# Delta rule and top-1 MoE: all 32 heads per chunk in tiled matmuls, with 16x16 diagonal blocks solved on GpSimd

## The chip, the cores and the metric

The kernel runs on one core of one Trainium2 chip. The metric is the device time of one execution in microseconds (us); lower is better. Everything is computed in float32 except the integer-valued lists of the selection, which use bfloat16. Engines are named as the profile names them: PE is TensorE (matmuls), PEld its weight loads, DVE VectorE, ACT ScalarE, POOL GpSimd, SP the SyncE queue that issues most transfers. "L269" is line 269 of the kernel.

## The reference

Two stages follow each other. The first is a delta-rule attention over 4 batches, 8 heads, 768 tokens and head dimension 48; the second a mixture of 8 experts, in which every token goes to its best expert and every expert keeps at most 80 tokens, those with the highest gate weight.

```
    k_n = k / (np.linalg.norm(k, axis=-1, keepdims=True) + 1e-06)
    state = np.zeros((B, H, D, D), dtype=np.float32)
    y = np.zeros_like(q)
    for t in range(S):
        kt, vt, bt = (k_n[:, :, t], v[:, :, t], beta[:, :, t, None])
        y[:, :, t] = np.einsum('bhd,bhde->bhe', q[:, :, t], state)
        v_old = np.einsum('bhde,bhd->bhe', state, kt)
        state = state + bt[:, :, :, None] * np.einsum('bhd,bhe->bhde', kt, vt - v_old)
    return y.astype(np.float32)

# ── moe block (D resized to bridge) ──
_moe_kname = 'topk_capacity_drop'
# ...
    x = np.ascontiguousarray(attn_out.transpose(0, 2, 1, 3)).reshape(B * S, H * D)   # 3072 x 384
    logits = x @ w_gate
    expert_idx = np.argmax(logits, axis=1)
# ... softmax; gate_w = probability of the chosen expert
    for e in range(E):
        tok_idx = np.where(expert_idx == e)[0]
        if len(tok_idx) > capacity:                  # capacity is 80
# ...       keep the 80 tokens with the largest gate_w
        h = np.maximum(x[tok_idx] @ w1[e], 0.0)      # 384 -> 1024
        out[tok_idx] = gate_w[tok_idx, None] * (h @ w2[e])   # 1024 -> 384
```

The loop over tokens is not run as a loop. Tokens are taken in chunks of 64. Within a chunk, with A[t, s] = beta_s k_t.k_s for s < t and S the 48x48 state of a head, the kernel solves Z = (I + A)^-1 (V - K S), sets U = beta Z, returns y = Q S + (Q K^T, s < t) U, and adds K^T U to S. So a chunk of one head needs the inverse of a 64x64 unit-triangular matrix, which does not depend on S, and a short chain of products that does.

## The kernel before

Two heads share a 128x128 tile, block-diagonal over the pair; a step handles one batch, one chunk, and its four pairs. There are 4 x 12 = 48 such steps, taken two at a time. The inverse comes from blocks that double in size: five rounds of two 128x128 matmuls and a transpose, each round with two or three evictions from PSUM (the accumulator memory of PE).

```
            for n in range(1, len(widths)):                  # widths 1, 2, 4, ..., 32
                pp = pm_tile()
                for p in range(NP):
                    nc.tensor.matmul(pp[:, p, :], lhsT=B1[:, p, :], rhs=X[:, p, :], start=True, stop=True)
                P2 = mtile("P2", 3)
                nc.vector.tensor_tensor(out=P2, in0=pp, in1=over_pairs(masks[n]), op=Alu.mult)
                yield
                if n < len(widths) - 1:
                    px = pm_tile()
                    for p in range(NP):
                        nc.tensor.matmul(px[:, p, :], lhsT=Y[:, p, :], rhs=P2[:, p, :], start=True, stop=True)
                    X = mtile("X")
                    nc.scalar.copy(X, px)
                    yield
                py = pm_tile()
                for p in range(NP):
                    if n < len(widths) - 1:
                        nc.tensor.transpose(py[:, p, :], X[:, p, :], ident)
                    else:
                        nc.tensor.matmul(py[:, p, :], lhsT=P2[:, p, :], rhs=Y[:, p, :], start=True, stop=True)
                Y = mtile("Y", 5)
                nc.scalar.copy(Y, py)
                yield
```

Ahead of it stand the transposes of K and Q and the two Gram products (L241, L246, L248), and after it the chain that depends on the state:

```
                for p in range(NP):
                    nc.tensor.matmul(ps[:, p, :], lhsT=KT[:, p, :], rhs=st[:, p, :], start=True, stop=True)
                R = vec.tile([128, NP, D], F32, name="R")
                nc.vector.tensor_tensor(out=R, in0=vin[b][:, :, c, :], in1=ps, op=Alu.subtract)
                yield
            ps = pc_tile()[:, :PD].rearrange("q (p d) -> q p d", p=NP)
            for p in range(NP):
                nc.tensor.matmul(ps[:, p, :], lhsT=Y[:, p, :], rhs=R[:, p, :], start=True, stop=True)
            U = vec.tile([128, NP, D], F32, name="U")
            nc.vector.tensor_tensor(out=U, in0=ps, in1=beta_t[:, b, :, c : c + 1].to_broadcast([128, NP, D]),
                                    op=Alu.mult)
            yield
            py = pc_tile()[:, :PD].rearrange("q (p d) -> q p d", p=NP)
            for p in range(NP):
                if c > 0:
                    nc.tensor.matmul(py[:, p, :], lhsT=QT[:, p, :], rhs=state[b][:, p, :], start=True, stop=False)
                nc.tensor.matmul(py[:, p, :], lhsT=PT[:, p, :], rhs=U[:, p, :], start=(c == 0), stop=True)
# ...                                              state += kb^T U (L322); y to DRAM as x_rows (L334)
            r = slice(C * (c % 2), C * (c % 2) + C)
            for n in range(NP):
                g, e = divmod(n, 2)
                nc.tensor.matmul(pl[r, :E], lhsT=xT[:, g, 64 * e : 64 * e + 64], rhs=wg[:, g, e, :],
                                 start=(n == 0), stop=(n == NP - 1))
            nc.vector.tensor_copy(lg[r, b * NT + c // 2, :], pl[r, :E])
```

When a batch is finished its gate weights are formed on DVE (L356 to L388), and the 80 largest of each expert are kept in lists. A list here is the tokens of one 128-token tile for one expert, 6 x 8 = 48 lists of 80 kept and 128 new values. After the last batch the 48 lists are brought to one row per expert by six transfers and searched again:

```
            for t in range(TR):
                m8 = nx[:, t * 8 : t * 8 + 8]
                nc.vector.max(m8, cd)
                nc.vector.match_replace(cd, in_to_replace=m8, in_values=cd, imm_value=0.0)
                if t % 2:
                    yield
# ... after the last batch
        mg = sl.tile([E, NT, CW], F32, name="mg")
        for t in range(NT):
            nc.sync.dma_start(mg[:, t, :], last[t * E : (t + 1) * E, :CW])
        top = sl.tile([E, CW], F32, name="top")
        mgf = mg.rearrange("e t w -> e (t w)")
        for t in range(TR):
            m8 = top[:, t * 8 : t * 8 + 8]
            nc.vector.max(m8, mgf)
            if t < TR - 1:
                nc.vector.match_replace(mgf, in_to_replace=m8, in_values=mgf, imm_value=0.0)
```

Then the rows of the chosen tokens are gathered by index, and the experts run one after the other. Each w1 and w2 is 1.5 MB. Four of the 16 are loaded early (WR0 = 4), six after the attention, the last six as slots come free:

```
    for e in range(E):
        w1_t, w2_t = w_t[2 * e], w_t[2 * e + 1]
        hT = fs.tile([128, FK, cap], F32, name="hT")
        for f0 in range(0, FK, TH):
            f1 = min(f0 + TH, FK)
            hp = ps_h.tile([128, 512], F32, name="hp")
            for f in range(f0, f1):
                for c in range(DK):
                    nc.tensor.matmul(hp[:, (f - f0) * cap : (f - f0 + 1) * cap],
                                     lhsT=w1_t[:, c, f * 128 : (f + 1) * 128], rhs=xTs[e][:, c, :],
                                     start=(c == 0), stop=(c == DK - 1))
            nc.scalar.activation(hT[:, f0:f1, :], hp[:, : (f1 - f0) * cap].rearrange("p (f t) -> p f t", t=cap), Act.Relu)
        load_w(2 * e + WR)
        tokens_in(e + 1)
        yp = ps_y.tile([128, 512], F32, name="yp")
        for f in range(FK):
            nc.tensor.matmul(yp[:cap, :DM], lhsT=hT[:, f, :], rhs=w2_t[:, f, :], start=(f == 0), stop=(f == FK - 1))
        load_w(2 * e + 1 + WR)
```

## Time and profile before

The median of three runs is 1165.03 us (1162.92 to 1165.09). The profiled execution spans 1162.0 us.

| stage | from, us | to, us | read from |
|---|---|---|---|
| loads, constants, norms, before the first transpose | 0 | 28.7 | timeline |
| attention, all chunks | 28.7 | 1013.2 | timeline |
| gate weights of the last batch | 1013.4 | 1019.6 | timeline |
| last lists of that batch | 1019.7 | 1028.3 | timeline |
| lists to one row per expert, by transfer | 1028.0 | 1036.8 | timeline |
| search for the 80th value, ten rounds | 1036.8 | 1050.3 | timeline |
| token indices | 1050.3 | 1060.7 | timeline |
| gather, first transposes | 1061.6 | 1066.3 | timeline |
| eight experts | 1066.3 | 1157 | timeline |

| engine | busy us | instructions |
|---|---|---|
| PE | 1056.7 | 8825 |
| DVE | 439.1 | 982 |
| ACT | 326.7 | 609 |
| POOL | 236.3 | 436 |

In the table of groups the columns are line, engine, operation, output and inputs, sizes and count; then busy time and the mean duration of one; then how long the engine had been idle just before, and what ended the idle time. A PE instruction is pipelined, so its duration is a latency; what it costs in a dense stream is the distance between two starts, which the timeline gives.

### The profile page before, as it was taken

Reading aid. Unit: us, or ns where it says so; the run is one execution under the profiler, and the core shown is the slowest. Engines: PE = TensorE matmul, PEld = TensorE weight load, DVE = VectorE, ACT = ScalarE, POOL = GpSimd, SP = SyncE. Lnnn points to the kernel's source line nnn. Section 1 sums busy time; section 2 is a strip of 40 time slices with the busy share of each in tenths; the row PEclk is TensorE's granted clock in tenths of the full one; section 3 lists DMA queues with packets and bytes.
Section 4 is the critical chain, followed back from the end, with each engine's and each line's share of the span. In section 5 each row is a group of like instructions: output and inputs, shape, how many; then the busy total and the mean of one; then the engine's idle time right before and its main releaser. Section 6 shows DMA issues by size and latency. Waiting matters only on the chain. (4 is left out here: it accounts for less than half of the span.)

```text
span 1162.0 us, 21302 instructions
## 1 busy us (share of the span) xinstructions
PE 1056.7 (91%) x8825; PEld 993.7 (86%) x8825; DVE 439.1 (38%) x982; ACT 326.7 (28%) x609; POOL 236.3 (20%) x436
## 2 busy tenths in 40 slices
PE   0799999999999999999999999999999999704998
PEld 0789999999999999999999999998999999704775
DVE  3352333433433624534335333344345323364010
ACT  1234223423322343333234223333332342100000
POOL 3320222032212202221220223023112201002000
PEclk9999999999999999999999999999999999755999
DMA  7930401400200005002000000000000000361820
GB/s 119 211 140 18 155 7 23 71 8 11 43 5 7 6 5 89 5 5 48 8 5 5 8 5 7 6 8 5 5 8 8 5 5 8 93 241 34 275 72 13
DMA packets 116863, 52.22 MB, mean 45 GB/s; under 512 B 103456, under 2 KB 111648, under 8 KB 116768
## 3 DMA queue, kind: packets, MB, share of 16 engines
q1 hardware_dynamic: 114720, 48.79, 17.8%
q0 software_dynamic: 768, 1.97, 0.6%
q8 instruction: 70, 1.15, 0.4%
q10 hardware_dynamic: 1280, 0.11, 0.1%
q14 instruction: 25, 0.20, 0.1%
HBM read 40.42 MB, written 10.42 MB: 44 GB/s over the span
## 5 line engine op out<-in xcount | busy, mean ns | idle before, releaser
L269 PE MATMUL pm<-X,B 128*128 128x128 f32 x1920 | 244.1, 281 | 3.6 <-DVE X L264 3.4
L269 PEld LDWEIGHTS pm<-X,B 128*128 128x128 f32 x1920 | 228.2, 195 | 8.9 <-DVE X L264 8.4
L271 DVE TENSOR_TENSOR P<-pm,mask 128x512 f32<-128x512 f32 x240 | 165.5, 690 | 172.7 <-PE pm L269 168.7
L278 ACT COPY X<-pm 128x512 f32<-128x512 f32 x192 | 112.4, 585 | 363.5 <-PE pm L276 363.4
L276 PE MATMUL pm<-P,Y 128*128 128x128 f32 x1536 | 195.4, 280 | 1.0 <-DVE ohg L388 0.5
L276 PEld LDWEIGHTS pm<-P,Y 128*128 128x128 f32 x1536 | 179.5, 191 | 9.3 <-issue 2.6
L287 ACT COPY Y<-pm 128x512 f32<-128x512 f32 x240 | 138.4, 588 | 104.7 <-PE pm L285 63.3
L283 PE MATMUL pm<-ident,X 128*128 128x128 f32 x768 | 117.4, 281 | 5.2 <-ACT X L278 3.5
L236 POOL COPY qbd<-qin 64x192 f32<-64x192 f32 x96 | 32.7, 342 | 387.8 <-PE pm L241 382.9
L283 PEld LDWEIGHTS pm<-ident,X 128*128 128x128 f32 x768 | 85.0, 145 | 16.2 <-ACT X L278 14.8
L234 POOL TENSOR_TENSOR kbd<-kin,inv 64x192 f32<-64x192 f32 x96 | 48.9, 509 | 220.3 <-PE pc L322 199.4
L318 PE MATMUL pc<-U,PT 128*128 128x48 f32 x384 | 73.0, 277 | 0.3 <-DVE U L311 0.2
L331 ACT COPY xs<-pc 128x192 f32<-128x192 f32 x48 | 15.3, 318 | 188.6 <-PE pc L318 188.3
L317 PE MATMUL pc<-st,QT 128*128 128x48 f32 x352 | 66.2, 270 | 0.0
L258 POOL TENSOR_TENSOR Y<-B,mask1T 128x512 f32<-128x512 f32 x48 | 60.9, 1269 | 4.0
L311 DVE TENSOR_TENSOR U<-pc,beta_t 128x192 f32<-128x192 f32 x48 | 17.2, 358 | 111.2 <-PE pc L309 111.2
L318 PEld LDWEIGHTS pc<-U,PT 128*128 128x128 f32 x384 | 58.3, 195 | 0.5 <-DVE U L311 0.5
L317 PEld LDWEIGHTS pc<-st,QT 128*128 128x128 f32 x352 | 54.4, 195 | 0.0
L246 PE MATMUL pm<-KT 128*128 128x128 f32 x384 | 53.1, 282 | 0.0
L248 PE MATMUL pm<-QT,KT 128*128 128x128 f32 x384 | 51.6, 278 | 0.0
L579 PEld LDWEIGHTS hp<-xTe,w 128*128 128x128 f32 x384 | 49.0, 210 | 2.1 <-issue 1.2
L285 PE MATMUL pm<-Y,P 128*128 128x128 f32 x384 | 49.0, 280 | 0.5
(153 smaller groups left out, 1232.8 us busy)
## 6 DMA issues: line engine op xcount, KB each, us to landing
w<-in_moe_w_dram SPq DMA_DIRECT2D x16, 1536.0 KB
kin<-in_k_dram SPq DMA_DIRECT2D x32, 144.0 KB
qin<-in_q_dram SPq DMA_DIRECT2D x32, 144.0 KB
vin<-in_v_dram SPq DMA_DIRECT2D x32, 144.0 KB
x_rows<-xs SPq DMA_DIRECT2D x96, 48.0 KB
out_dram<-zero SPq DMA_DIRECT2D x12, 384.0 KB
bt<-in_beta_dram ACTq DMA_DIRECT2D x32, 3.0 KB
wg<-in_moe_w_gate_dram ACTq DMA_DIRECT2D x8, 1.5 KB
```

What stands on the lines that cost most here:

```text
L246: nc.tensor.matmul(pk[:, p, :], lhsT=KT[:, p, :], rhs=KT[:, p, :], start=True, stop=True)
L248: nc.tensor.matmul(pq[:, p, :], lhsT=KT[:, p, :], rhs=QT[:, p, :], start=True, stop=True)
L258: nc.gpsimd.tensor_tensor(out=Y, in0=B1, in1=over_pairs(mask1T), op=Alu.mult)
L269: nc.tensor.matmul(pp[:, p, :], lhsT=B1[:, p, :], rhs=X[:, p, :], start=True, stop=True)
L271: nc.vector.tensor_tensor(out=P2, in0=pp, in1=over_pairs(masks[n]), op=Alu.mult)
L276: nc.tensor.matmul(px[:, p, :], lhsT=Y[:, p, :], rhs=P2[:, p, :], start=True, stop=True)
L278: nc.scalar.copy(X, px)
L283: nc.tensor.transpose(py[:, p, :], X[:, p, :], ident)
L285: nc.tensor.matmul(py[:, p, :], lhsT=P2[:, p, :], rhs=Y[:, p, :], start=True, stop=True)
L287: nc.scalar.copy(Y, py)
L317: nc.tensor.matmul(py[:, p, :], lhsT=QT[:, p, :], rhs=state[b][:, p, :], start=True, stop=False)
L318: nc.tensor.matmul(py[:, p, :], lhsT=PT[:, p, :], rhs=U[:, p, :], start=(c == 0), stop=True)
```

## The change

The attention is rewritten around a different unit of work, and the stages after it are adapted.

1. **All heads per chunk.** A step is now one chunk of 64 tokens of all 32 heads of all four batches: 12 steps in sequence in place of 48. Products are no longer padded to block-diagonal 128x128 tiles. They address a quarter of the PE array (64 rows by 64 columns, for one head) or a half (128 rows, a stacked pair of heads, by 64 columns), and the emission alternates between quarters.
2. **The inverse.** The four 16x16 diagonal blocks of every head's 64x64 matrix (128 blocks, one per partition) are written to DRAM, fetched with one block per partition, inverted on POOL by back substitution in 14 pairs of elementwise operations, written to DRAM again, and spread into block-diagonal tiles XB and YB. Two merging levels on PE (16 to 32, 32 to 64) replace five rounds.
3. **Fixed order.** The order of every engine's instructions in the attention is written by hand instead of left to the scheduler. Inverses are built one to four chunks ahead of the chain; small DVE work (norms, gates, lists) fills chosen gaps.
4. **List selection.** 24 lists of 256 new values in place of 48 of 128; the final lists are brought to one row per expert by PE transposes in place of transfers, and the search runs over 240 values a row in place of 480.
5. **Experts.** Each 128-column weight tile of the first product is split into two 64-column tiles. A burst of bfloat16 matmuls stands ahead of the first expert. No expert weight is loaded before the attention ends (WR0 = 0).

```diff
 # unit of work
-            for dst, src in ((KT, kb), (QT, qb)):
-                pt = pm_tile()
-                for p in range(NP):
-                    nc.tensor.transpose(pt[:, p, :], src[:, p].rearrange("q e w -> q (e w)"), ident)
-                nc.scalar.copy(dst, pt)
+        HEADS = [(e, p, g) for e in range(2) for p in range(2) for g in range(NQ)]
+        # tiles(): emits one product per quarter of the array in turn:
+            order = [kk for kk in ((0, 0), (1, 1), (0, 1), (1, 0)) if kk in cls]
+            for n in range(max(len(x) for x in cls.values())):
+                for kk in order:
+                    if n < len(cls[kk]):
+                        emit(*cls[kk][n])
+        # trans(): K and Q of a pair, 8 transposes each
+                for g in range(NQ):
+                    nc.tensor.transpose(pt[:, g // 4, (g % 4) * 128 : (g % 4) * 128 + 128],
+                                        src[:, 2 * g : 2 * g + 2, :].rearrange("r p d -> r (p d)"), ident)
+                for h in range(2):
+                    nc.scalar.copy(KQs[c][:, 4 * h : 4 * h + 4, n, :], pt[:, h].rearrange("r (g w) -> r g w", w=128))
 # Gram products in quarter tiles: K K^T and K Q^T in one matmul
+            for h in range(2):
+                ps = mtile()
+                tiles(lambda e, p, g: (p, e),
+                      lambda e, p, g: mm(ps[hs(e), p, 128 * (g % 4) : 128 * (g % 4) + 128].rearrange("r (k w) -> r k w", k=2),
+                                         KQ[hs(p, D), g, 0, hs(e)], KQ[hs(p, D), g, :, hs(e)]),
+                      [hd for hd in HEADS if hd[2] // 4 == h])
 # ... evicted by DVE with the masks
 # inverse
-                pp = pm_tile()
-                for p in range(NP):
-                    nc.tensor.matmul(pp[:, p, :], lhsT=B1[:, p, :], rhs=X[:, p, :], start=True, stop=True)
-                P2 = mtile("P2", 3)
-                nc.vector.tensor_tensor(out=P2, in0=pp, in1=over_pairs(masks[n]), op=Alu.mult)
+        # store(): B1 to a_dram (two transfers); fetch():
+                NTs[c] = sml.tile([128, 16, 16], F32, name="NT")
+                eng.dma_start(NTs[c], a_dram[c % 2].rearrange("(s z) -> s z", z=PB)[:, :1024]
+                                    .rearrange("s (r w) -> s r w", w=64)[:, :, :16])
+        # solve():
+            eng.tensor_tensor(out=X, in0=NT.rearrange("p s t -> p t s"), in1=eye16, op=Alu.add)
+            for t in range(14, 0, -1):
+                sh = [128, 15 - t, t]
+                tmp = sml.tile([128, 64], F32, name=f"tmp{eng is nc.gpsimd}")
+                tv = tmp[:, : (15 - t) * t].rearrange("p (c s) -> p c s", s=t)
+                eng.tensor_tensor(out=tv, in0=X[:, t + 1 :, t : t + 1].to_broadcast(sh),
+                                        in1=NT[:, 0:t, t].unsqueeze(1).to_broadcast(sh), op=Alu.mult)
+                eng.tensor_tensor(out=X[:, t + 1 :, 0:t], in0=X[:, t + 1 :, 0:t], in1=tv, op=Alu.add)
+            eng.tensor_copy(XY[:, 1], X.rearrange("p t s -> p s t"))
+        # spread(), spread_t():
+            nc.sync.dma_start(i_dram[c % 2][:, :], Xss.pop(c).rearrange("p k c s -> p (k c s)"))
+            src = i_dram[c % 2].rearrange("(e m i) (k c s) -> e i k c m s", e=2, i=4, k=2, s=16)
+            for e in range(2):
+                for i in (0, 2):
+                    r = 64 * e + 16 * i
+                    engs[e].dma_start(XB[r : r + 16, :, e, 16 * i : 16 * i + 16], src[e, i, 0])
+            src = i_dram[c % 2].rearrange("(m h i) (k c s) -> h i k c m s", h=2, i=4, k=2, s=16)
+            for i in range(4):
+                for h in range(2):
+                    r = 64 * h + 16 * i
+                    eng = nc.scalar if c < 2 and h else nc.sync
+                    eng.dma_start(YB[r : r + 16, :, h, 16 * i : 16 * i + 16], src[h, i, 1])
 # merging levels
+                B1, ps = B1s[c], mtile()
+                for n in range(2):
+                    nc.tensor.matmul(ps[:, n, :], lhsT=identb, rhs=eyes.rearrange("r g w -> r (g w)"), start=True, stop=False,
+                                     skip_group_check=True)
+                for p, g in PAIRS:
+                    mm(ps[hs(g // 4), p, 128 * (g % 4) : 128 * (g % 4) + 128].rearrange("r (e w) -> r e w", e=2),
+                       B1[:, slot(p, g)], XB[:, slot(p, g)], acc=True)
+                P2 = P2s[c] = one.tile([128, 2, 4, 2, 64], F32, name="P2")
+                for p in range(2):
+                    nc.vector.tensor_tensor(out=P2[:, p].rearrange("r g e w -> r (g e) w"), in0=ps[:, p].rearrange("r (g w) -> r g w", w=64),
+                                            in1=mask.unsqueeze(1).to_broadcast([128, 8, 64]), op=Alu.mult)
+        # merge_x4, merge_y4, merge_p5, merge_y5: products of 64x32 (32 of them), 64x128 (16), 32x32 (32), 64x64 (32)
 # chain: ks (16 products of 64x96), tr (32 of 64x48), qs, ku, pu (16 each of 64x96 or 48x96)
+                ps, KQ = mtile(), KQs[c]
+                for e, g in PAIRS:
+                    mm(ps[hs(g // 4), e, 2 * D * (g % 4) : 2 * D * (g % 4) + 2 * D].rearrange("r (p d) -> r p d", p=2),
 # the loop, in the fixed order
+        for j in range(NC):
+            if j % GC == GC - 1 and j > GC:
+                gate_pool(j // GC - 1)
+            if j > 0:
+                scale_k(j + 4)
+            beta_mask(j + 4)
+            spread(j + 2)
+            if j == 0:
+                chain(j)
+                both(j + 4)
+            if j > 0:
+                chain_ks(j)
+            if j % 2 == 0:
+                fillers.insert(0, newton(squares([j + 5, j + 6])))
+            merge_x4(j + 1)
+            if j > 0:
+                chain_tr(j)
+            merge_y4(j + 1)
+            spread_t(j + 2)
+            fill(0.5)
+            merge_p5(j + 1)
+            fetch(j + 3)
+            solve(j + 3)
+            if j > 0:
+                chain(j)
+            load_k(j + 7)
+            load_q(j + 5)
+            load_v(j + 2)
+            if j < zr.shape[0]:
+                nc.sync.dma_start(zr[j], zero.unsqueeze(1).to_broadcast([128, 2, DM]))
+            fill(7.0 if j < NC - GC else 8.0 - 2 * (j % GC))
+            merge_y5(j + 1)
+            if j > 0:
+                both(j + 4)
+            merge_p2(j + 2)
+            out_t(j)
+            gram(j + 4)
+            logits(j)
 # weights
-    WR0, WR = 4, 10
+    WR0, WR = 0, 10
 # lists to one row per expert
-            nc.sync.dma_start(mg[:, t, :], last[t * E : (t + 1) * E, :CW])
+        nc.tensor.transpose(lt_ps[:CW, : NL * E], last[:, :CW], ident[: NL * E, : NL * E])
+        lt = sl.tile([CW, NL * E], F32, name="lt")
+        nc.vector.tensor_copy(lt, lt_ps[:CW, : NL * E])
+        mg_ps = ps_l.tile([128, 512], F32, name="mg_ps")
+        for t in range(NL):
+            nc.tensor.transpose(mg_ps[:E, t * CW : t * CW + CW], lt[:, t * E : t * E + E], ident[:CW, :CW])
+        nc.vector.tensor_copy(mg.rearrange("e t w -> e (t w)"), mg_ps[:E, : NL * CW])
+        for i in range(WR0, WR):
+            load_w(i)
 # experts
+    wm = ps_y.tile([128, 512], F32, name="yp")
+    for _ in range(12):
+        nc.tensor.matmul(wm, lhsT=identb, rhs=eyes.rearrange("r g w -> r (g w)"), start=True, stop=True)
+    tokens_in(0)
 # ...
+            for f in range(f0, f1):
+                for c in range(DK):
+                    for n in range(2):
+                        r = slice(64 * n, 64 * n + 64)
+                        nc.tensor.matmul(hp[r, (f - f0) * cap : (f - f0 + 1) * cap],
+                                         lhsT=w1_t[:, c, f * 128 + 64 * n : f * 128 + 64 * n + 64], rhs=xTs[e][:, c, :],
+                                         start=(c == 0), stop=(c == DK - 1), skip_group_check=True)
+            nc.scalar.activation(hT[:, f0:f1, :], hp[:, : (f1 - f0) * cap].rearrange("p (f t) -> p f t", t=cap), Act.Relu)
```

## The prediction

> **What bounds the kernel now.** I read the page's busy line and its 40 slices first. PE is busy in 91% of the span; in slices 2 to 34 it is never below seven tenths, at a granted clock of 90% or more, while no other engine exceeds 38%. Then the table of groups by form, for what PE does and what the other engines' operations cost. Then the timeline of one attention stretch and of the tail.
>
> ```profile
> PE 1056.7 (91%) x8825; PEld 993.7 (86%) x8825; DVE 439.1 (38%) x982; ACT 326.7 (28%) x609; POOL 236.3 (20%) x436
> ...
> PE   0799999999999999999999999999999999704998
> ...
> PEclk9999999999999999999999999999999999755999
> ```
>
> ```profile
> L269 PE MATMUL pm<-X,B 128*128 128x128 f32 x1920 | 244.1, 281 | 3.6 <-DVE X L264 3.4
> ...
> L271 DVE TENSOR_TENSOR P<-pm,mask 128x512 f32<-128x512 f32 x240 | 165.5, 690 | 172.7 <-PE pm L269 168.7 <-issue 3.1
> L287 ACT COPY Y<-pm 128x512 f32<-128x512 f32 x240 | 138.4, 588 | 104.7 <-PE pm L285 63.3 <-PE pm L283 37.3
> L283 PE MATMUL pm<-ident,X 128*128 128x128 f32 x768 | 117.4, 281 | 5.2 <-ACT X L278 3.5
> ...
> L258 POOL TENSOR_TENSOR Y<-B,mask1T 128x512 f32<-128x512 f32 x48 | 60.9, 1269 | 4.0
> ...
> L408 DVE MAX8 cand<-cand 48x8 f32<-48x208 f32 x40 | 14.7, 368 | 1.2
> ...
> L489 DVE MAX8 top<-mg 8x8 f32<-8x480 f32 x10 | 6.5, 649 | 8.9 <-DMA mg<-cand 8.5
> ```
>
> DVE and ACT waited for PE (L271, L287); PE waited for almost nothing. L269 shows a counting rule: 48 steps x 4 pairs x 5 rounds are 960 matmuls, but 1920 instructions, so a float32 matmul is two. A transpose is one (L283: 48 x 4 x 4 = 768). The price is the distance between starts:
>
> ```profile
> 216.70 0.63 PE L347 MATMUL pc<-wg,xT 96*64 96x8 f32 x8
> 217.26 2.05 PE L269 MATMUL pm<-X,B 128*128 128x128 f32 x16
> 219.30 2.02 PE L276 MATMUL pm<-P,Y 128*128 128x128 f32 x16
> ```
>
> Sixteen instructions in 2.04 us is 127 ns each with the group's own ends; between single starts the trace's median is 112 ns. L347, with 64 weight columns, has 58 ns between starts. The 128-column products with only 48 moving columns (L322) also take 112 ns: the weight load sets the pace, and half the columns cost half.
>
> The tail, from the last logits at 1013.2 to the end, is a separate 149 us: 52.8 us until the first expert matmul at 1066.3, one expert started cold (16 us), seven at 10.7 us each, then the last scatter.
>
> **What the Trainium skill says.** (1) "TensorE: Matmul & The Clock Gate", section "LDWEIGHTS (loading the stationary operand)": the time is columns / 1.2 in ns, whatever the number of rows, so 107 and 53. The trace agrees, with some 5 ns added (112 and 58). (2) The same page, "Part 3: Packing small matmuls": products in different row groups run concurrently and their weight loads overlap. No run here shows it yet; it is the main unknown. (3) "GPSIMD Engine Reference", section "Elementwise — side-by-side cycle accounting": about 2.6 cycles per element for two inputs at 1.2 GHz. The trace agrees: 1269 ns at 512 elements and 292 ns at 48 give 2.1 ns per element plus 190 ns. (4) "DMA: Bandwidth & Descriptors", section "Specifications": transfers below 512 B run below line rate. The trace agrees: a 192-byte packet of k, q or v took 20 ns on average, a 4096-byte packet of weights 175 ns.
>
> **Part 1, PE work of the attention.** Removed: about 8200 instructions between 28.7 and 1013 us, 120 ns each. Added, per step: 22 transposes (16 for K and Q, 6 for x); 2 bfloat16 fills of 512 columns; and float32 products, two instructions each: gram 32, p2 16, x4 32, y4 16, p5 32, y5 32, ks 16, tr 32, qs 16, ku 16, pu 16, logits 12. That is 268 products, 536 instructions. Transposes cost 22 x 0.109 = 2.4 us, the fills about 0.4. If the quarters do not overlap, 536 x 0.058 = 31.1, so 34 us per step. If everything overlaps to 30 ns (an assumption), 16.1, so 19 us. I choose 40 ns: the emission alternates row groups on purpose, and the experts were split from 24 matmuls of 128 columns into 48 of 64, which is worth writing only below 56 ns. That gives 21.4 + 2.8 = 24.2 us.
>
> **Part 2, the other engines in a step.** From the rows above, an eviction of 512 elements is 0.69 us on DVE and 0.59 on ACT, scaled with size. DVE: gram 4 x 0.69, p2 2 x 0.69, p5 0.55, R 2 x 0.56, U 2 x 0.96, logits 0.16; and per step, averaged, norms 2.4, gates 1.9, lists 3.8: 16 us. ACT: KQ 4 x 0.6, x4 and p5 0.6 each, y4 and Y 1.2 each, state and x 0.9 each, xT 0.8, squares 0.9: 9.5 us, plus three transfer issues. POOL: 28 solve operations with 1120 elements, 28 x 0.19 + 1120 x 0.0021 = 7.7, its two end operations 1.1, key scaling of 768 elements 1.8, beta mask of 1024 elements 2.3: 13 us. SP issues 22 transfers of about 0.6 us (x_rows and k loads take 0.55 and 0.65): 13 us, and waits in between. Packets: about 6100 of 192 B at 20 ns, 4100 of 256 B or less from store and fetch, 3100 of 64 B spread at about 12 (between the 8 ns of 32-byte and the 20 of 192-byte packets), and the larger rows, about 270 us over 16 engines: 17 us. All lie under 24 us, beside PE. Walking the fixed order, I find PE waiting about 2 us per step, where the two K/Q tiles and the small PSUM ring (three buffers) make it wait for ACT. So 26 us per full step.
>
> **Part 3, the loop.** The last four steps have no K/Q and gram work (4 x 4.8 = 19 us), the last ones no merges (13), the first no ks (1); the last chain is exposed (+4). 12 x 26 - 19 - 13 - 1 + 4 = 283 us.
>
> **Part 4, the start.** Loads now take 2 transfers per tensor and chunk instead of 8 per batch, so the first K arrives at about 6 us. Norm, scaling, transposes and gram end near 20 us; then come a DRAM round trip (5), a solve on DVE (30 operations, 5), another round trip (5), and the merges (12). With two more solves in the same queues I take 52 us before the loop.
>
> **Part 5, the tail.** Gate of the last batch unchanged, 6.2. Lists: MAX8 costs 1.03 ns per element more between 208 and 480, so at 336 elements 0.50; with the replacement a round is 1.13 instead of 0.86, and ten are 11.3 instead of 8.6. The six transfers (8.8) become transposes and two copies, 1.8. Ten rounds at 240 instead of 480 elements: 9.4 instead of 13.5. Indices and gather unchanged, 10.4 and 5.5. Sum 44.6 against 52.8. Experts: the first product is 96 instructions at 40 ns, 3.8, instead of 48 at 112, 5.4; 10.7 - 1.5 = 9.2 us, eight times, 74, with no cold start. End 5. Tail 124.
> All weights (25.2 MB) now come after the attention. At the 325 GB/s measured at 1010 to 1030 us that is 78 us, in the order of use; the first pair is needed 45 us after the start, the last at about 110. I count it hidden, with little room.
>
> Sum: 52 + 283 + 124 = 459 us.
>
> **The rivals.** A: no overlap, 58 ns. PE then takes 34 us per step, the loop 365 and the experts 10.7 each: about 550. For it: 58 ns is the only 64-column figure measured. B: full overlap, 30 ns. Then ACT and DVE evictions in the fixed order bind at about 21.5 us: loop 234, tail 116, total 403. C: the serial path of the inverses, gram, DRAM, POOL solve, DRAM, spread, falls behind the step, because SP runs 22 issues in order and waits for solves and for PE. A POOL operation on rows of 1 to 14 elements may cost more than the size model says. A step of 30 us or more would follow, total about 505. Against it: each hop has a step of lead. D: smaller products or short stalls leave PE at a lower granted clock, as in slices 35 to 37 (7, 5, 5); a loop at half the clock would reach 650 or more. Against it: PE has no idle stretch of that length in the order. E: the weights arrive late, up to +15 us.
>
> **Range and chances.** I weigh full overlap, 40 ns and no overlap about equally, with C and D drawing upwards: 459 us, 390 to 550. Even the worst of these is far below 1165, so faster by over 2% has 0.985, same 0.01, slower 0.005.
>
> **What would show it.** Right: PE starts in L208 about 40 ns apart, steps about 26 us apart, DVE near 190 us in the loop, POOL below PE, first expert 45 us after the last logits. Rival A shows as 58 ns, C as PE waiting for XB or YB by DMA, D in the clock row, E as PE waiting for w. I am wrong if the start takes over 70 us, or if one engine's fixed order stalls all others.

## The result, and the profile after

The changed kernel takes 434.4 us (median of four runs, 430.0 to 436.9) against 1164.0 us for the kernel before. The ratio is 0.372, with a 95% interval of 0.370 to 0.374. The prediction was 459 us, range 390 to 550. All profile lines of the changed kernel below are from the execution of 430.0 us, whose span is 428.3 us; it is the fastest of the four.

First the page: the busy line, the row of PE and of its granted clock in 40 slices, and one row of the table of transfer queues (packets, MB, share of the transfer engines' time).

```profile
PE 336.3 (79%) x7655; PEld 277.6 (65%) x7669; DVE 234.6 (55%) x614; ACT 118.8 (28%) x209; POOL 168.6 (39%) x415
...
PE   6657778989877989998999888898200249999995
...
PEclk9886899999998899999999998999755559999999
...
q8 instruction: 60, 0.98, 0.9%
```

PE is still the busiest engine, but no longer alone: DVE has risen from 38% to 55%. The first five slices are the start, slices 29 to 33 the list selection and the gather. The row q8 looks like nothing, 0.9% of the transfer time. It turns out to matter, so keep it in mind: 60 packets of 16 KB, which carry PE's own instructions.

Of the table by windows, the loop and the stretch from the last logits to the first expert (window, its length, then busy time of PE, PEld, DVE, ACT and POOL with counts, the granted clock, the share of the transfer engines, GB/s):

```profile
61.00:303.00 242.00, 214.51 (x6018) 192.75 (x6030) 143.12 (x343) 94.46 (x164) 119.37 (x325) 0.98 0.59 122
303.00:349.00 46.00, 5.87 (x43) 3.65 (x41) 32.89 (x107) 0.00 (x0) 7.78 (x14) 0.53 0.95 365
```

The loop runs at nearly full clock with PE busy in most of it; in the stretch after it DVE works, PE hardly does, and the weights arrive. The stages against the prediction:

| stage | predicted us | measured us |
|---|---|---|
| start, before the loop | 52 | 61 |
| loop of 12 chunks | 283 | 242 |
| tail, last logits to the end | 124 | 125 |
| sum | 459 | 428 |

So the prediction is 31 us above this execution (25 above the median), and two errors partly cancel: the loop is 41 us shorter and the start 9 us longer than predicted. The start of this execution is on the short side: the first logits came at 81.9 us, while four kernels that differ only behind that point (experts of 128 columns, w2 stationary, late burst, lists of 128) had them at 83.8 to 85.5.

The rows by form that answer to those shown of before:

```profile
L601 DVE MAX8 cand<-cand 24x8 f32<-24x336 f32 x40 | 20.0, 499 | 1.4
...
L386 DVE TENSOR_TENSOR P<-pm,mask 128x512 f32<-128x512 f32 x24 | 15.5, 685 | 34.0 <-PE pm L208 34.0
...
L806 DVE MAX8 top<-mg 8x8 f32<-8x240 f32 x10 | 4.0, 399 | 0.3
```

An eviction of 512 elements costs on DVE what it did (685 ns). What changed is how many there are: 24 of P in place of 240. The two searches cost 499 and 399 ns an operation, as worked out from the widths (0.50 for the first).

The timeline of PE within one step, at full clock (start, length of the group, then the group and its count):

```profile
153.70 1.14 PE L208 MATMUL pm<-P,YB 64*64 64x32 f32 x64
154.65 1.00 PE L208 MATMUL pm<-R,Y 64*64 64x48 f32 x36
156.36 0.67 PE L208 MATMUL pm<-R,Y 64*64 64x48 f32 x28 [0.70 <-issue]
...
161.75 1.49 PE L208 MATMUL S_ps<-UB,kn 128*48 128x96 f32 x32
163.07 1.49 PE L208 MATMUL pm<-UB,PT 128*64 128x96 f32 x32
164.50 1.16 PE L208 MATMUL pm<-Y,P 64*64 64x64 f32 x64
165.59 1.09 PE L301 MATMUL pm<-ident,kn 128*128 128x128 f32 x8
```

Read the distance from one group's start to the next. The 64 quarter tiles of P,YB take 0.95 us, 15 ns each; those of Y,P take 1.09 us, 17 ns each. The half tiles (all 128 rows, 64 columns) take 41 ns with 96 moving columns (1.32 / 32) and 55 with 128 (YB,P, the mean distance inside a group that does not stop); with the 8 moving columns of the logits it is 29. So their price grows with the moving columns. No group of quarter tiles shown is near the 40 ns that I chose, or the 58 ns of the kernel before. And one group, R,Y, stops in its middle for 0.70 us with the releaser "issue", which means that no semaphore explains it.

To compare runs I split each step in two: work is the sum of the distances between successive PE starts, each cut at 130 ns (240 for the 512-column fills), and stall is what exceeds that. The table is the mean of the first seven steps after the first logits, from one execution of each kernel, with the TensorE clock that was granted over these steps (1 is full speed).

| kernel | work us | stall us | step us | clock |
|---|---|---|---|---|
| changed kernel | 18.9 | 3.2 | 22.1 | 0.98 |
| no alternation | 29.9 | 1.9 | 31.9 | 0.91 |
| row pairs | 21.3 | 1.5 | 22.8 | 1.00 |
| y4 twice | 21.2 | 2.8 | 24.0 | 0.96 |
| short solve | 19.2 | 3.5 | 22.7 | 0.95 |
| order of SP | 19.3 | 3.3 | 22.5 | 0.96 |

No run holds the clock fixed, and between 1.00 and 0.95 lies up to 1.1 us of a step of 22, so small differences in this table can be the clock's.

Without the 22 transposes (2.5 us) and the two fills (0.45) the changed kernel's work is 16.0 us for 536 instructions: 30 ns each on average.

### The profile page after: what moved, and what is told of

Read it like the earlier page. It is cut to its first block, busy times and chain, and to the rows that moved or that the text cites. A ratio compares the mean times of both kernels' runs of the same rounds, so it can differ in the third digit from the quotient of the medians.

```text
span 428.3 us, 17433 instructions
## 1 busy us (share of the span) xinstructions
PE 336.3 (79%) x7655; PEld 277.6 (65%) x7669; DVE 234.6 (55%) x614; ACT 118.8 (28%) x209; POOL 168.6 (39%) x415
## 5 line engine op out<-in xcount | busy, mean ns | idle before, releaser
L350 POOL TENSOR_TENSOR tmpTrue<-XY,NT 128x14 f32<-128x14 f32 (+6 forms) x140 | 40.0, 286 | 11.0
L909 PE MATMUL yp<-w,hT 128*80 128x384 f32 x128 | 42.7, 487 | 0.0
L352 POOL TENSOR_TENSOR XY<-XY,tmpTrue 128x14 f32<-128x14 f32 (+6 forms) x140 | 37.5, 268 | 11.0
L208 PE MATMUL pm<-SB,KQ 128*64 128x96 f32 x704 | 35.3, 254 | 1.9 <-DVE lg L517 1.5
L386 DVE TENSOR_TENSOR P<-pm,mask 128x512 f32<-128x512 f32 x24 | 15.5, 685 | 34.0 <-PE pm L208 34.0
L208 PEld LDWEIGHTS pm<-SB,KQ 128*64 128x64 f32 x704 | 31.2, 141 | 3.3 <-PE pm L594 2.0
L901 PEld LDWEIGHTS hp<-xTe,w 128*64 128x64 f32 x768 | 29.1, 143 | 5.2 <-issue 4.9
L909 PEld LDWEIGHTS yp<-w,hT 128*80 128x80 f32 x128 | 18.5, 150 | 19.5 <-issue 19.3
L901 PE MATMUL hp<-xTe,w 128*64 128x80 f32 x768 | 30.4, 241 | 0.8 <-issue 0.7
L208 PE MATMUL pm<-KQ 48*64 48x128 f32 x768 | 26.1, 285 | 6.0 <-ACT KQ L304 4.0
L208 PE MATMUL pm<-YB,P 128*64 128x128 f32 x384 | 26.6, 291 | 4.5 <-issue 4.5
L481 ACT COPY SB<-S_ps 48x768 f32<-48x768 f32 x22 | 17.5, 793 | 28.2 <-PE S_ps L208 21.1
```

Of the source, the lines that this page charges most:

```text
L208: nc.tensor.matmul(out, lhsT=lhsT, rhs=rhs, start=not acc, stop=not acc, skip_group_check=True)
L350: eng.tensor_tensor(out=tv, in0=X[:, t + 1 :, t : t + 1].to_broadcast(sh), in1=NT[:, 0:t, t].unsqueeze(1).to_broadcast(sh), op=Alu.mult)
L352: eng.tensor_tensor(out=X[:, t + 1 :, 0:t], in0=X[:, t + 1 :, 0:t], in1=tv, op=Alu.add)
L386: nc.vector.tensor_tensor(out=P2[:, p].rearrange("r g e w -> r (g e) w"), in0=ps[:, p].rearrange("r (g w) -> r g w", w=64), in1=mask.unsqu ...
L481: nc.scalar.copy(SB[hs(p, D), :, :, p].rearrange("r (b g) e d -> r b (g e) d", b=2), S_ps[hs(p, D), :, : 8 * D].rearrange("r b (g d) -> r ...
L901: nc.tensor.matmul(hp[r, (f - f0) * cap : (f - f0 + 1) * cap], lhsT=w1_t[:, c, f * 128 + 64 * n : f * 128 + 64 * n + 64], rhs=xTs[e][:, c, :],
```

## The experiments

**No alternation.** The products of a group are emitted quarter by quarter, not in turn. This undoes one line of the change and leaves every product in place. Only the quarter tiles pass through these lines; the half tiles keep their order.

```diff
-            for n in range(max(len(x) for x in cls.values())):
-                for kk in order:
-                    if n < len(cls[kk]):
-                        emit(*cls[kk][n])
+            for kk in order:
+                for hd in cls[kk]:
+                    emit(*hd)
```

> Main theory: the quarters overlap only because consecutive products address different quarters, in weight loads and in streaming. With all products of one quarter in a row, the 64-column instructions of x4, tr and y5 fall back from about 16 ns to the 58 ns of a 64-column load, gram from 27 to 58, p5 (32 columns) from 10 to about 31: 64 x (0.042 x 3 + 0.031 + 0.021) = 11 us more PE work per step, the step from 22 to about 32 us, the time from 434 to 530 to 560. Rival: PE looks far enough ahead in its queue to overlap them in any order; then under 10 us more, 434 to 445.

Measured: 550.7 us (549.4 to 556.4), ratio 0.474 (0.472 to 0.477). The order of emission, with all that follows from it, is worth 116 us. In the timeline, a group of YB,P at half clock and then, again at full clock, the 64 products of Y,P:

```profile
149.54 3.68 PE L207 MATMUL pm<-YB,P 128*64 128x128 f32 x32
...
163.03 3.40 PE L207 MATMUL pm<-Y,P 64*64 64x64 f32 x64
166.36 1.09 PE L300 MATMUL pm<-ident,kn 128*128 128x128 f32 x8
```

The products of Y,P take 3.33 us, 52 ns each, where they took 17. A step is 31.9 us. Part of its growth is not the order itself: the granted clock fell from 0.98 to 0.91, with PE never stopped in the middle of a group, which is up to 2.9 us of the step (0.09 x 31.9) against 0.4 before. Rival A of the prediction had the time that comes without overlap (550) about right, though not by its own sum, and was wrong that there would be no overlap.

**Which direction overlaps.** Two quarters at a time, those that differ in rows (row pairs) or in columns (column pairs).

```diff
-            order = [kk for kk in ((0, 0), (1, 1), (0, 1), (1, 0)) if kk in cls]
-            for n in range(max(len(x) for x in cls.values())):
-                for kk in order:
-                    if n < len(cls[kk]):
-                        emit(*cls[kk][n])
+            for pair in (((0, 0), (1, 0)), ((0, 1), (1, 1))):       # row pairs
+            #           (((0, 0), (0, 1)), ((1, 0), (1, 1)))        # column pairs
+                order = [kk for kk in pair if kk in cls]
+                for n in range(max(len(cls[kk]) for kk in order)):
+                    for kk in order:
+                        if n < len(cls[kk]):
+                            emit(*cls[kk][n])
```

> Only two quarters alternate at a time, those that differ in their rows (first the pair on the left half of the columns, then the pair on the right half). 320 of the 536 instructions of a step are quarter tiles; with all four quarters in turn they start 10 to 18 ns apart, and with none in turn the whole kernel took 551 us. Main theory: both directions overlap, each giving a factor of about two, so a quarter tile would start every 29 ns or so, 320 x 13 ns = 4 us more per step, of which about 1.5 us falls into waits that are there anyway: 455 to 475 us. Rival: only row groups run beside each other[...], and this order loses nothing: 432 to 440 us.

> Only two quarters alternate at a time, those that share their rows and differ in their columns. Main theory (both directions count about equally): 455 to 475 us, as with the row pairs. Rival (only row groups overlap): hardly better than no alternation, 535 to 550 us. Second rival (columns alone give it all, as the half tiles suggest, which never differ in rows): 432 to 440 us.

Measured: row pairs 444.0 us (440.1 to 445.6), ratio 0.380 (0.378 to 0.382). The column pairs took 446.8 us in one execution, and in the other three 456.4 to 461.3, slow ones at a lower granted clock, so there is no ratio. The group of Y,P, with its successor for the row pairs, which come first; the line of the column pairs is from a stretch at full clock of the execution of 461.3 us:

```profile
172.36 1.91 PE L209 MATMUL pm<-Y,P 64*64 64x64 f32 x64
174.20 0.98 PE L302 MATMUL pm<-ident,kn 128*128 128x128 f32 x7
```

Column pairs:

```profile
151.99 1.91 PE L209 MATMUL pm<-Y,P 64*64 64x64 f32 x64
```

The group is as long, to its successor 1.84 us in both, 29 ns a product. So 52, 29, 29 and 17 ns for none, rows, columns and both: each direction gives a factor of 1.7 to 1.8, and the mechanism of the main theory is right for both. The Trainium skill says in "TensorE: Matmul & The Clock Gate", "Part 3: Packing small matmuls", that a weight load runs beside matmuls only when the row group differs, though the table of the same section has column tiles gain too. Here pairs that differ only in columns gained as much as pairs that differ only in rows: 29 ns in both.

The time of the row pairs was missed, though: I expected 455 to 475 us. PE's work grows by 2.3 us per step, but its stalls shrink by 1.7 (3.2 to 1.5), and the step grows by only 0.7. Two thirds of the slowing of the products cost nothing. About half of the 1.7 us are the stops that no semaphore explains (1.15 us a step in the changed kernel, 0.3 with row pairs); the section after the experiments comes back to them. The rest are waits for other engines, and the full clock of the row pairs helped by up to 0.4 us.

**One product group twice.** The 16 products of y4 are issued twice in a row, with the same result.

```diff
-                            mm(ps[hs(p), e, ...], P2[:, p, ql, e], YB[:, 8 * e + 4 * p + ql])
+                            for _ in range(2):
+                                mm(ps[hs(p), e, ...], P2[:, p, ql, e], YB[:, 8 * e + 4 * p + ql])
```

> Every product of the 64x64 level that uses all 128 rows (y4, 16 products, 32 instructions a step) is issued twice in a row; the result is the same. Main theory: PE's own instructions bound the loop, so the extra 32 x 54.5 ns = 1.74 us comes through in each of the 12 steps but for what falls into waits: 446 to 456 us. Rival: the evictions on DVE and ACT in their fixed order set the step and PE has slack: 434 to 440 us.

Measured: 450.2 us, ratio 0.385 (0.383 to 0.387). Of the 20.9 us added (12 x 1.74), 15.7 come through. PE sets the loop; DVE and ACT in their fixed order leave it little slack that more PE work could use up.

**Is it the path of the inverses?** Two runs. In the first the back substitution does 4 of its 14 pairs of operations (10 pairs are left out, so the inverses are incomplete). In the second SP issues the write of the inverse ahead of the loads of q, v and the zero fill, which in the changed kernel stood before it.

```diff
-            for t in range(14, 0, -1):
+            for t in range(14, 10, -1):
```

> Leaves out 10 of the 14 pairs of the solve (20 POOL operations of some 0.28 us, 5.6 us per step; in the start 20 DVE operations of 0.23 us in each of two solves). Main theory: the loop is bound by PE work, with stalls of 1 to 4 us a step that only partly come from late inverses: loop 5 to 15 us shorter, start about 5 to 8 shorter, 412 to 424. Rival (the serial path of the inverses sets the step): the loop loses 5 us per step, 375 to 390. Second rival (nothing waits for the inverse): only the start gains, 426 to 430.

```diff
             nc.sync.dma_start(i_dram[c % 2][:, :], Xss.pop(c).rearrange("p k c s -> p (k c s)"))
+            j = c - 3
+            if j >= 0:
+                load_q(j + 5)
+                load_v(j + 2)
+                nc.sync.dma_start(zr[j], zero.unsqueeze(1).to_broadcast([128, 2, DM]))
```

> The q, v and zero transfers of a step are issued after the inverse is written out instead of ahead of it. Main theory: the inverse leaves late because SP issues in order and stands behind these five loads (6.7 us at one place of the trace), and PE's waits for XB go away: 8 to 15 us shorter, 419 to 426. Rival: SP is full in any order and the wait moves to YB or to the spread itself: 430 to 437.

Measured: 433.9 us, ratio 0.372 (0.371 to 0.373), for the short solve; 437.5 us, ratio 0.375 (0.374 to 0.376), for the order of SP. Neither gained, and my main theory fell in both. For the short solve none of the three ranges holds: not even the start gained (see part 4 below). For SP the rival came close (430 to 437). The busy line of the short solve shows that the work was really gone from POOL:

```profile
PE 341.4 (79%) x7655; PEld 284.7 (66%) x7669; DVE 230.7 (53%) x574; ACT 118.9 (27%) x209; POOL 111.3 (26%) x215
```

57 us less on POOL, nothing less in the time, and PE's stalls as before. What looked like PE waiting for the end of a long serial path was not that. Rival C's 5 us per step are excluded by this; a gain of some tenths per step is not, because the clock was lower in this execution (0.95 against 0.98). For SP, the list of waits of its queue in the reordered kernel has one entry that answers for the missing gain:

```profile
SPq L358 <- POOL XY L353: 54.9, 9, 10.9
```

It was 16.8 us in the changed kernel. Issued first, the write of the inverse makes SP stand still until POOL is done, and the loads behind it wait instead.

**The experts.** First the split into 64 columns undone, then the split applied to the second product as well, with w2 as the stationary side and three transposes back.

```diff
-                    for n in range(2):
-                        r = slice(64 * n, 64 * n + 64)
-                        nc.tensor.matmul(hp[r, ...], lhsT=w1_t[:, c, f * 128 + 64 * n : f * 128 + 64 * n + 64], ...)
+                    nc.tensor.matmul(hp[:, ...], lhsT=w1_t[:, c, f * 128 : (f + 1) * 128], ...)
```

> Main theory: the first expert product costs its PE time in full, 96 half-width instructions at 37 ns (3.5 us) against 48 at 112 ns (5.4 us), so undoing the split adds 1.85 us for each of eight experts: 449. Rival: the experts follow the arrival of the weights, and the period of 9.0 us stays: 434 to 437.

```diff
-        for f in range(FK):
-            nc.tensor.matmul(yp[:cap, :DM], lhsT=hT[:, f, :], rhs=w2_t[:, f, :], start=(f == 0), stop=(f == FK - 1))
+        for d in range(DK):
+            for f in range(FK):
+                for n in range(2):
+                    nc.tensor.matmul(yT[64 * n : 64 * n + 64, d * cap : (d + 1) * cap],
+                                     lhsT=w2_t[:, f, d * 128 + 64 * n : d * 128 + 64 * n + 64], rhs=hT[:, f, :], ...)
+        nc.scalar.copy(yS, yT[:, : DK * cap].rearrange("p (d t) -> p d t", t=cap))
+        for d in range(DK):
+            nc.tensor.transpose(yp[:cap, d * 128 : (d + 1) * 128], yS[:, d, :], ident)
```

> A version that may be better: in the second product of an expert w2 is the stationary side in 64-column tiles, as w1 is, and the result is transposed back by three transposes after a copy on ACT. Main theory: 96 instructions at 37 ns, 3.55 us, plus 0.33 for the transposes and about 0.5 of waiting for the copy, in place of 5.33 us: period 8.0 instead of 9.0 us, 425 to 429 us. Rival: the copy, the transposes and the second PSUM tile make PE wait about a microsecond per expert: 432 to 437 us.

Measured: 450.0 us, ratio 0.385 (0.383 to 0.388), without the split; 425.9 us (424.3 to 427.5), ratio 0.365 (0.364 to 0.366), with w2 stationary. Both as expected, and the second beats the changed kernel. The first product in the undone kernel, then both products of an expert of the changed kernel, then the second product and its transposes with w2 stationary:

```profile
379.69 5.48 PE L899 MATMUL hp<-xTe,w 128*128 128x80 f32 x48
```

```profile
369.57 3.54 PE L901 MATMUL hp<-xTe,w 128*64 128x80 f32 x96
...
373.30 5.33 PE L909 MATMUL yp<-w,hT 128*80 128x384 f32 x16
```

```profile
366.39 3.54 PE L911 MATMUL yp<-hT,w 128*64 128x80 f32 x96
...
370.39 0.53 PE L919 MATMUL yp<-ident,yS 128*80 128x128 f32 x3
```

96 products of 64 columns take 3.5 us in either role, 37 ns each; 48 of 128 take 5.4; 16 of 384 moving columns take 5.3. The period falls from 10.7 to 9.0 to 8.0 us.

**The warm-up burst.** In the changed kernel the 12 bfloat16 matmuls written ahead of the first expert did not run there:

```profile
289.12 1.46 PE L889 MATMUL yp<-eyes,identb 128*128 128x512 bf16 x5
...
292.90 0.81 PE L889 MATMUL yp<-eyes,identb 128*128 128x512 bf16 x3 [0.16 <-issue]
```

Their inputs are constants, so the scheduler outside the hand-ordered part put them into gaps of the last attention steps, 55 us early. The first expert then started at half clock. The experiment ties them to the gate weights:

```diff
+    late = fs.tile([cap, 512], BF16, name="late", bufs=1)
+    nc.vector.tensor_copy(late, gw_t[:, 0:1].to_broadcast([cap, 512]))
     for _ in range(12):
-        nc.tensor.matmul(wm, lhsT=identb, rhs=eyes.rearrange("r g w -> r (g w)"), start=True, stop=True)
+        nc.tensor.matmul(wm, lhsT=identb[:cap, :], rhs=late, start=True, stop=True)
```

> The 12 bfloat16 matmuls meant to raise the clock ahead of the first expert ran at 289 to 295 us, between the last steps of the attention, because nothing tied them to their place. Here their moving side is made from the gate weights of the chosen tokens, so they can't start before the indices are ready. Main theory: they fill the 6 us of waiting for the gather, the first expert starts at full clock (first product 3.5 us in place of 5.9, so 2.2 us less), and the last steps of the attention lose up to 1 us of foreign work: 430.5 to 433 us. Rival: the burst is no help, because the clock is given back later than it lasts (12 x 0.43 us at half clock), or because it delays the first transposes: 434 to 436 us.

Measured: 432.7 us (431.0 to 437.6), ratio 0.372 (0.371 to 0.373). The median lies in the range of the main theory, but the ratio is that of the changed kernel, and the trace shows that the theory failed:

```profile
342.58 5.30 PE L891 MATMUL yp<-late,identb 80*128 80x512 bf16 x12 [1.43 <-DVE late L889]
348.46 1.06 PE L881 MATMUL xp<-ident,xg 80*128 80x80 f32 x6 [0.58 <-issue]
349.62 3.79 PE L903 MATMUL hp<-xTe,w 128*64 128x80 f32 x48
354.28 1.91 PE L903 MATMUL hp<-xTe,w 128*64 128x80 f32 x48 [0.87 <-issue]
```

The burst now stands where it was meant to, and still the first 48 products take 3.79 us and the next 48 take 1.91. The granted clock came back at 353.8 us, in the changed kernel at 353.6, where PE had begun only at 347.8. A burst of 5.3 us and a pause of 0.58 did not bring it back earlier. Whether the pause or the kind of work is to blame was not tried.

**The beta mask in the start.** In the changed kernel an operation of the first solve on DVE, usually 0.21 us, takes as long as a POOL operation beside it:

```profile
33.64 1.90 POOL L292 TENSOR_TENSOR bm<-beta_t,neg_strict 128x1024 f32<-128x1024 f32 x1
33.72 1.89 DVE L352 TENSOR_TENSOR XY<-XY,tmpFalse 128x50 f32<-128x50 f32 x1
```

```diff
-        beta_mask(3)          # ahead of both(2)
         ...
         solve(2)
+        beta_mask(3)
```

> In the start the beta mask of chunk 3 on POOL (1.90 us) lies beside the solve of chunk 0 on DVE, and one of its operations, 0.21 us elsewhere, took 1.89 us until the mask was done. Here the mask is formed after the solve of chunk 2. Main theory: a DVE operation on SBUF data waits for the POOL operation that runs, so the solve of chunk 0 ends 1.7 us earlier, and so does the first logits: 431.5 to 433.5 us, and no DVE operation of that solve over 0.3 us. Rival: the hold only hides another wait (the transfers of XB and YB, the solve of chunk 1 ahead of the first P eviction), and the time stays: 434 to 436 us.

Measured: 441.2 us, ratio 0.380 (0.379 to 0.382): slower. The mechanism was right:

```profile
33.68 0.21 DVE L352 TENSOR_TENSOR XY<-XY,tmpFalse 128x50 f32<-128x50 f32 x1
```

The same operation is 0.21 us without the mask beside it, and the first solve ends at 36.1 instead of 37.9 us. The gain reached PE at first: its second group of the merges, P,YB, started at 47.8 instead of 49.5. But I had chosen a bad place. POOL's own solve of chunk 2 waits for its blocks until 52 us, so the mask came at 63.9, and PE waited for the Gram eviction that needs it:

```profile
67.15 0.61 PE L379 MATMUL pm<-eyes,identb 128*128 128x512 bf16 x1 [10.86 <-DVE PT L324]
```

Moved behind a wait of its engine, the mask inherited the wait (63.9 us in place of 33.6). Whether the 1.7 us would last to the end with the mask in a better place was not tried.

**All three together.** The late burst, the later mask and the stationary w2 in one kernel.

> The late burst, the later mask and the stationary w2 together, a version that may be better. If the three add up (-2.5, -1.7, and -8.5 as measured for w2): 421 to 423 us. If the weights now come too late for the faster experts, or the clock falls elsewhere: 424 to 428 us.

Measured: 439.0 us, ratio 0.377 (0.376 to 0.378), worse than w2 alone. It fits neither expectation. The first logits came at 93.5 us, where the kernel with w2 alone had them at 85.5: the misplaced mask again. The best version measured is w2 stationary alone.

**Lists of 128 again.** 48 lists and a search over 480 values, as before the change, but brought together by transposes.

```diff
-    NL = 3
+    NL = 6
```

> Only the list selection is undone in its widths: 48 lists of 128 new values and a final search over 480, still brought together by transposes. From the rows of the kernel before: ten rounds of lists 8.6 in place of 11.3 us, six transposes in place of three +0.3, search 13.5 in place of 9.4: 1.7 us more in the tail; in the loop the list work on DVE falls from 34 to 26 us a run, which counts only if DVE sets the step. Main theory (DVE doesn't): 435.5 to 437.5 us. Rival (shorter fillers free the step): 429 to 433 us.

Measured: 435.2 us, ratio 0.374 (0.373 to 0.374), against 0.372 (0.370 to 0.374): no difference that these runs resolve, just under the range of the main theory and outside that of the rival. In its trace the stretch from the last logits to the token indices is 40.0 us (306.7 to 346.7) against 37.3 (303.1 to 340.4), 2.7 more where I expected 1.7.

## What stops PE in the middle of a group

Three facts needed one cause: stalls without a semaphore; no gain from lighter POOL or SP work; slower products that cost little. The list of PE's waits from 80 to 310 us (total, times, longest) puts the largest sum on no engine; the second line, for comparison, is the one wait for the gate of the last batch:

```profile
PE pm L208 <- issue: 8.4, 10, 2.2
PE pm L594 <- DVE ohg L572: 5.6, 1, 5.6
```

I set these stops beside the packets of queue q8. "Trainium Architecture — The Big Picture", section "The software stack", says that instructions are 64 bytes each, so a 16 KB packet holds 256. The profile agrees: 7655 matmuls and 7669 weight loads in 60 packets are 255 a packet. Every stop of over 0.45 us, from the first logits on, inside a group that had all its data, from the trace of the changed kernel:

| stop at us | for us | matmul number | since the last stop | resumes after a packet landed, us |
|---|---|---|---|---|
| 86.90 | 1.51 | 1350 | | 1.47 |
| 110.88 | 1.26 | 1981 | 631 = 5 x 126 | 1.41 |
| 132.72 | 2.51 | 2485 | 504 = 4 x 126 | 1.53 |
| 155.44 | 0.92 | 2988 | 503 = 4 x 126 | 1.33 |
| 159.95 | 0.60 | 3116 | 128 | 1.43 |
| 184.25 | 0.70 | 3747 | 631 = 5 x 126 | 1.30 |
| 199.39 | 1.01 | 4123 | 376 = 3 x 125 | 1.45 |
| 219.82 | 0.56 | 4627 | 504 = 4 x 126 | 1.41 |
| 242.75 | 1.29 | 5258 | 631 = 5 x 126 | 1.34 |
| 352.09 | 1.05 | 6789 | 1531 = 12 x 128 | 1.38 |

The stops lie a whole number of packets apart (126 matmuls, as many weight loads, and a few other instructions make 256), and PE resumes 1.3 to 1.5 us after a packet has landed. The short solve, the reordered SP and the w2 kernel stop at the same matmuls (1350, 1981, 2485, 2988, 5258), whatever POOL and SP do. Nor is it the place in the program: with y4 twice, the stops are still whole packets apart (1349, 1981, 2612, 3747), though other products stand there (1981 is in R,Y, where it was in X,B). What fits all of this is that PE waits for its own instructions.

In the loop of the kernel before, a packet was needed every 14.7 us and there was not one such stop. In the changed kernel one is needed every 5.0 us on average, and at 15 ns a product the 126 products of a packet last 2 us, while a packet takes about 1.0 us to move and the transfer engines also carry q, k, v, the inverses and the rest. Row pairs spread the demand, and their mid-group stops add up to 4.0 us in place of 10.4; without alternation there is none. So, if this is the cause, the overlap that the change is built on creates the wait that eats part of it: about 0.9 us per step in the loop directly. Some stops may cost more: after that of 132.72 the clock is at half until 142.

```profile
135.24 0.70 PE L208 MATMUL pm<-YB,P 128*64 128x128 f32 x4 [2.24 <-issue]
...
136.87 2.83 PE L208 MATMUL pm<-SB,KQ 128*64 128x96 f32 x32
139.48 2.71 PE L208 MATMUL S_ps<-UB,kn 128*48 128x96 f32 x32
142.02 1.49 PE L208 MATMUL pm<-UB,PT 128*64 128x96 f32 x32
```

The last two groups do the same number of products, in 2.71 us at half clock and in 1.49 at full. But a stop neither always does this nor is needed for it: with lists of 128 the same stop (2.51 us at 134.0) was followed by full clock, and without alternation PE ran at half clock from 144.9 to 161.9 with no stop before. What sets the clock is not shown here. The account of the stops rests on the alignment of stops and packets in the traces. No run changed the fetching itself, so how much the time would fall without it stays open.

## Why the prediction was right, and where it was not

The mechanism was right: PE was the bound, the rewriting takes most of its work away, and what is left overlaps. By its steps:

- **Part 1, "I choose 40 ns".** This is the term that was mis-sized. The average is 30 ns, rival B's figure: quarter tiles at 9 to 27 ns, half tiles at 40 to 55. PE's work is 18.9 us a step in place of 24.2. My argument from the experts' split bounded the price of half tiles only (they are at 37 ns). It said nothing of quarters, which are 320 of the 536 instructions.
- **Part 1, the waits.** I took 2 us per step and blamed the PSUM ring and ACT. It is 3.2, and a third of this goes to the stops that fit instruction supply, which I had not thought of.
- **Rival B.** It had the rate and the step (21.5 against 22.1), but not the cause: it let evictions bind. DVE is busy 86.9 of 155.0 us in the seven steps, and added PE work came through.
- **Part 2.** Single operations were as worked out: evictions 0.69 and 0.59, the solve 7.75 us plus 1.5 for its ends, scaling 1.48 (I took 1.8), beta mask 1.90 (2.3). DVE is at 143 us in the loop, not 190: my average per step held work that runs in the start (norms and Gram evictions of the first chunks, in its 50.9 us) and in the tail (the last gate and lists).
- **Part 3.** 242 us in place of 283, from the rate of part 1: 5.3 us a step less work, 1.2 more waiting.
- **Part 4.** 61 us in place of 52. Every link of the chain was longer than I took it: the first trip through DRAM 9.4 us (18.8 to 28.2) in place of 5, the first solve on DVE 9.6 (to 37.9) in place of 5, the second trip 7.0 (to 44.9) in place of 5, the merges 16 in place of 12, some of them at half clock. But the long solve alone is not to blame. In the short solve it was done at 33.6, 4.3 us earlier; SP, still issuing loads of k, wrote the inverse out only 0.8 us earlier, and PE began its first merge 0.5 us earlier. The write and the merge, changed kernel first:

```profile
37.89 0.61 SPq L358 DMA_DIRECT2D inv_blocks<-XY  x1
44.90 1.97 PE L208 MATMUL pm<-XB,B 128*64 128x128 f32 x32 [0.19 <-DMA XB<-inv_blocks]
```

```profile
37.09 1.10 SPq L358 DMA_DIRECT2D inv_blocks<-XY  x1
44.41 3.68 PE L208 MATMUL pm<-XB,B 128*64 128x128 f32 x32 [4.64 <-DMA XB<-inv_blocks]
```

So in the start, what rival C feared for the loop did happen: SP's order and the trips through DRAM hold PE. No run shortened the trips.

- **Part 5.** 45.9 us from the last logits to the first expert (predicted 44.6) and 9.0 us per expert (9.2). The gather took 5.6 us from issue to the first transposes, against 3.1 in the kernel before, while the transfers ran at 312 GB/s. "With no cold start" was wrong: the first half of the first product ran at half clock, the burst ran elsewhere, and the late burst shows that in its place it did not help either.
- **Rival C** (path of the inverses, 5 us or more per step in the loop) was refuted by the short solve; PE waited for XB by transfer once in the loop, 2.4 us. **D** (clock) is small in the loop of the changed kernel (0.98 granted), but not without alternation (0.91). **E** (late weights): PE waited for no weights.

The range held because no overlap and full overlap were both inside it, and the centre was between them. The total looks better than its parts: the loop was off by 41 us.

## What to carry to other kernels

Small products on PE overlapped in rows and in columns, but only where neighbours in the stream lay in different quarters: write the order by hand and read the distance between starts. Once products take 15 ns, ask what feeds PE, since its own instructions arrive by transfer too, 60 packets here. A warm-up burst of constants runs wherever the scheduler likes, so look for it in the timeline before you count on it.

## What the runs showed of the hardware

- Quarter tiles in float32 with 64 moving columns started every 52 ns when neighbours lay in the same quarter, every 29 when they alternated in rows or in columns, every 17 with both.
- PE stopped for 0.56 to 2.51 us in the middle of groups, whole packets of 256 instructions apart, and resumed 1.3 to 1.5 us after an instruction packet landed.
- A DVE operation on SBUF inputs took 1.89 us in place of 0.21 while a POOL operation with two inputs (1.90 us) ran beside it, and 0.21 again without it.
- After a stop of 2.51 us PE ran at half clock for about 7 us (135 to 142); after an equal stop in another kernel it did not, and without alternation it ran at half clock for 17 us with no stop before. A bfloat16 burst of 5.3 us did not bring the clock back.
